# A fused attention and two-MLP kernel: centred tiles turned by VectorE through DRAM, the second MLP ordered behind the next block's first, and bulk transfers issued from GpSimd's queue

## The chip, the cores and the metric

The kernel runs on one NeuronCore of a Trainium2 chip. The metric is the device time of one execution in microseconds (us), lower is better. Matrix products run on TensorE (PE in the profile, its weight loads PEld), elementwise work on VectorE (DVE) and ScalarE (ACT), a little on GpSimd (POOL), and transfers are issued by SyncE (SP). In the kernel before, every transfer is issued by SP.

## The reference

```python
scores = (1 / S) * z @ z.T                     # per batch, B = 2, S = 3136, d_qk = 64
x = u * (relu(scores) ** 2 @ v)                # d_model D = 256
h = relu(x @ w_in)                             # first MLP, d_ff = 1024
c = conv over 3 neighbouring rows of h, one weight per column (conv_w)
x = (h * sigmoid(c)) @ w_out
xn = (x - mean(x)) / sqrt(var(x) + 1e-6) * g_ln    # second MLP
out = x + relu(xn @ w_ch1) @ w_ch2             # 4 * 256 = 1024 wide
```

Inputs and output are float32.

## The kernel before

Every float32 operand is split into a high and a low part (names that end in `h` and `l`), and a product is three matmuls: high by high, high by low, low by high. PE is the engine with the most work.

Attention runs over 14 chunks of 3 or 4 tiles of 128 queries (7 for each batch), and within a chunk over 25 tiles of 128 keys. A score tile `s` is computed by PE, made to `a` by ACT (relu, square), split into `ah` and `al`, and used by six `av` matmuls. Scores are symmetric, so a tile whose mirror image was computed in an earlier chunk is not computed again: `spill` turned it with a DVE transpose into a buffer `bl` and wrote it to a DRAM tensor `turned`, and `land` reads it back in four transfers. Each finished chunk is multiplied by `u` and written to a DRAM tensor `gated` (`x out`).

The MLPs run over 17 blocks of tokens, 15 of 3 x 128 and two of 2 x 128. For each block, `make_x` loads a stretch of `gated` into a tile `x` (`x in`), and ACT and DVE split it into `xh` and `xl`, of which there is one buffer each. `mlps` then issues, for eight slices of d_ff, the `up` matmuls into `hps`, the convolution and the gate on ACT and DVE, and the `down` matmuls into the PSUM tile `y`. The result is copied to `ysb`; the mean and variance come from bn_stats, each row tile is centred into `xn` (`center`), PE turns the six 128 x 128 pieces of `xn` into the PSUM tile `tps` by matmuls with the identity (`turn`, 6 instructions), and ACT and DVE scale them into `xth` and `xtl`. The second MLP is again eight slices of `up` (into `h2ps`) and `down` (into `y`), and the rows are written out. The reciprocal root is applied after the second MLP and runs on POOL (`pow`).

The order of the instructions on each engine is not the order of the code. `Program` records every operation with its engines, a price and a due time, plays them through with those prices, picks the most urgent one that is ready and has room in its buffers, and issues the result. The order is then fixed: every engine, and every queue of transfers, runs its list from the front, and an instruction that has to wait holds up what stands behind it. `when` gives the due times of a block, `LAG0` and `LAG1` how far it lies behind its attention. Where the plan has a gap on PE of over 0.1 us, `fill` puts matmuls on zeros (`warm_ps<-zero`, or `y<-zero` and `av<-zero` where they add zero to a sum), one for each 0.125 us.

Of the kernel before, what the change touches and what calls it, by code (L numbers as in the profile page):

```python
# [8 lines left out]
F32 = mybir.dt.float32  # L9
# [20 lines left out]
LAG0 = 120.0  # L30
LAG1 = 6.0
# [12 lines left out]
REST = 0.9  # L44
FLOAT = ("ACT", "POOL")
# [48 lines left out]
class Program:  # L94
# [62 lines left out]
    def order(self):  # L157
# [17 lines left out]
        done, now, port, owner, moved_at = [], 0.0, 0.0, None, 0.0  # L175
        busy = dict.fromkeys(ENGINES, 0.0)
        while len(done) < len(self.ops):
# [32 lines left out]
            for e in ENGINES:  # L210
# [4 lines left out]
                for o in open_[e]:  # L215
# [3 lines left out]
                    if (e == "POOL" or e == "DVE" and o.port) and port > now + 1e-9 and owner != e:  # L219
                        later(port)  # L220
                        continue
# [22 lines left out]
                if o.kb is not None:  # L244
                    moved_at = max(moved_at, now + us) + o.kb / RATE
                    o.end = moved_at + LANDS + LATE.get(o.name, 0.0)
                if e == "POOL" or e == "DVE" and o.port:
                    port, owner = now + us + 0.06, e
# [49 lines left out]
def attn_moe_kernel(ctx: ExitStack, tc: tile.TileContext, zt, ut, v, w_in, conv_w, w_out, g_ln, w1, w2, out):  # L298
# [28 lines left out]
    def maker(tag, places, where, shape, dtype):  # L327
# [7 lines left out]
        for tag, places, where, shape, dtype in (  # L335
            ("zst", 1, pool, [P, 512], F32),
            ("st", 2, pool, [P, 1024], F32),
            ("bl", 4, pool, [P, CW], F32),
# [10 lines left out]
            ("x", 1, pool, [P, 2 * XW], F32),  # L349
# [6 lines left out]
            ("ysb", 1, pool, [P, NTT * D], F32),  # L356
            ("xn", 3, pool, [P, D], F32),
# [49 lines left out]
    def dma(fn, kb, **kw):  # L407
        return op([("SP", 0.45)], lambda e: fn(), late=LANDS + kb / RATE, kb=kb, **kw)
# [14 lines left out]
    def load_z(b, i, with_lh=None):  # L423
# [3 lines left out]
        dma(lambda: nc.sync.dma_start(out=at(st, "zst")[:, :n], in_=zt[b, :, c0:c1]), n / 2, reads=held(b), writes=[(st, 0)], name="z1" if b else "z")  # L427
# [25 lines left out]
    def load_v(b, j0, j1):  # L453
        st = buf("st")
# [6 lines left out]
        if full > j0:  # L461
            dma(
                lambda: nc.sync.dma_start(
# [3 lines left out]
                128 * (full - j0), reads=held(b), writes=[(st, 0)], name="v1" if b else "v",  # L467
            )
            keys.append((st, 0))
        if j1 == NJ:  # L470
            for o in (0, 64):
                dma(
                    lambda o=o: nc.sync.dma_start(out=tile_()[o : o + 64, full - j0, :], in_=v[b, full * P : S, :]),
                    64, writes=[(st, 1 + o)], name="v",
# [67 lines left out]
    def load_w(nm, i):  # L542
        st = buf("st")
# [5 lines left out]
        def start():  # L549
            if nm in ("wi", "w1"):  # L550
                k, o = divmod(i * 512, DFF)
                nc.sync.dma_start(out=words(), in_=wsrc[nm][:, k, o : o + 512, :])
            else:
                nc.sync.dma_start(
# [10 lines left out]
    def load_cw():  # L565
# [3 lines left out]
            lambda: nc.sync.dma_start(out=at(st), in_=conv_w.bitcast(U32).rearrange("p (n two) -> p n two", two=2)),  # L569
# [10 lines left out]
    def swap_lh(c):  # L580
# [5 lines left out]
        dma(lambda: nc.sync.dma_start(out=f(at(b, "lh")[:64, :n]), in_=f(hl[64:, q0:q1])), 96, reads=keys, writes=[(b, 0)], name="lh")  # L586
# [650 lines left out]
```

## Time and profile before

| | |
|---|---|
| median of 3 runs | 1100.31 us (1099.48 to 1100.45) |
| the profiled execution | 1099.48 us; its span, first to last instruction, 1097.7 us |
| PE busy | 1086.1 us, 99% of the span |
| DVE / ACT / POOL busy | 78% / 66% / 3% of the span |
| granted TensorE clock | full throughout (2.4 GHz) |
| moved by DMA | 115.43 MB, mean 105 GB/s |

Busy time on PE is time in which a matmul is in flight; successive matmuls overlap, so the time that one costs is the distance from its start to the next one's, which is shorter than its duration. A wait is put down to the instruction whose end came last before the waiting one began.

### The profile page before, as it was taken

How to read it: one execution, taken by the hardware profiler on the slowest of the kernel's cores; microseconds unless marked ns; L12 is line 12 of the kernel's file. 1: busy time of each engine (PE TensorE's matmuls, PEld its weight loads, DVE VectorE, ACT ScalarE, POOL GpSimd, SP SyncE). 2: the span in 40 equal slices, each digit the busy share in tenths (PEclk: the TensorE clock that was granted, in tenths of full speed). 3: DMA queues.
4: the chain of work that ended last, by engine and by line, in shares of the span. 5: the costliest groups of instructions: out<-in, count | busy, mean ns of one | idle time of the engine just before them, and what ended most of it. 6: DMA issues, size and time to landing. Idle time of an engine off the chain costs nothing.

```text
span 1097.7 us, 19194 instructions
## 1 busy us (share of the span) xinstructions
PE 1086.1 (99%) x6641; PEld 1023.4 (93%) x6641; DVE 858.9 (78%) x1820; ACT 723.7 (66%) x1506; POOL 32.2 (3%) x48
## 2 busy tenths in 40 slices
PE   8999999999999999999999999999999999999998
PEld 7888988989999989899989999999899999999998
DVE  7999999988778696869694959595849668487973
ACT  7778887865657595858584857484747557355752
POOL 2000000000000000000000000000000000000000
PEclk9999999999999999999999999999999999999999
DMA  6775888776557431213142413340534545450000
GB/s 202 227 197 148 200 184 179 162 161 135 98 134 151 139 88 44 82 44 103 35 106 69 116 37 87 79 91 26 112 87 96 130 84 94 109 83 27 25 15 20
DMA packets 373793, 115.43 MB, mean 105 GB/s; under 512 B 277312, under 2 KB 365376, under 8 KB 373696
## 3 DMA queue, kind: packets, MB, share of 16 engines
q1 hardware_dynamic: 373696, 114.21, 44.2%
q8 instruction: 52, 0.85, 0.3%
q14 instruction: 45, 0.37, 0.1%
HBM read 64.74 MB, written 46.47 MB: 101 GB/s over the span
## 4 chain that ended last, share of the span: by engine, by line
PE 91%; ACT 3%; DVE 2%; DMA 1%; issue 1%; SPq 1%; DVEq 0%; ACTq 0%
PE av L755 12%; PE av L758 12%; PE av L757 11%; PE y L856 8%; PE y L858 8%; PE y L857 8%; PE hps L840 4%; PE h2ps L840 4%; PE hps L841 4%; PE h2ps L842 4%; PE h2ps L841 4%; PE hps L842 4%; PE s L714 3%; PE s L713 3%; PE tps L1014 1%
## 5 line engine op out<-in xcount | busy, mean ns | idle before, releaser
L755 PE MATMUL av<-ah,vh 128*128 128x512 f32 (+2 forms) x700 | 257.8, 368 | 2.9 <-ACT ah L397 1.1
L758 PE MATMUL av<-ah,vl 128*128 128x512 f32 (+2 forms) x700 | 256.0, 366 | 0.0
L757 PE MATMUL av<-al,vh 128*128 128x384 f32 (+2 forms) x672 | 246.7, 367 | 2.2 <-DVE al L692 2.1
L1047 DVE SCALAR_TENSOR_TENSOR g2l<-h2ps,g2h 128x384 fp32r<-128x384 f32 (+1 forms) x136 | 73.3, 539 | 101.2 <-ACT g2h L1042 100.7
L1042 ACT ACTIVATE g2h<-h2ps 128x384 fp32r<-128x384 f32 (+1 forms) x136 | 65.3, 481 | 130.0 <-PE h2ps L842 128.4
L755 PEld LDWEIGHTS av<-ah,vh 128*128 128x128 f32 x700 | 131.6, 188 | 15.1 <-ACT ah L397 1.8
L758 PEld LDWEIGHTS av<-ah,vl 128*128 128x128 f32 x700 | 131.5, 188 | 14.6
L757 PEld LDWEIGHTS av<-al,vh 128*128 128x128 f32 x672 | 126.4, 188 | 14.0 <-DVE al L692 3.9
L722 ACT ACTIVATE a<-s 128x512 f32<-128x512 f32 (+2 forms) x196 | 106.0, 560 | 38.6 <-PE s L714 37.9
L692 DVE TENSOR_TENSOR al<-a,ah 128x512 fp32r<-128x512 f32 (+2 forms) x182 | 114.8, 639 | 9.4 <-ACT ah L397 8.8
L856 PE MATMUL y<-w2h,g2h 128*128 128x256 f32 x392 | 110.0, 281 | 0.6 <-DVE ysb L1057 0.6
L856 PE MATMUL y<-woh,gh 128*128 128x256 f32 x392 | 109.8, 280 | 0.2 <-ACT ysb L948 0.2
L858 PE MATMUL y<-w2h,g2l 128*128 128x256 f32 x392 | 109.7, 280 | 0.0
L858 PE MATMUL y<-woh,gl 128*128 128x256 f32 x392 | 109.7, 280 | 0.0
L857 PE MATMUL y<-w2l,g2h 128*128 128x256 f32 x392 | 109.7, 280 | 0.0
L857 PE MATMUL y<-wol,gh 128*128 128x256 f32 x392 | 109.6, 280 | 0.0
L692 DVE TENSOR_TENSOR al<-land,ah 128x384 fp32r<-128x384 f32 (+2 forms) x154 | 92.3, 600 | 21.7 <-ACT ah L397 16.2
L731 ACT ACTIVATE a<-a 128x512 f32<-128x512 f32 (+2 forms) x183 | 105.8, 594 | 1.4
L397 ACT CAST ah<-a 128x512 fp32r<-128x512 f32 (+2 forms) x181 | 104.2, 587 | 3.3 <-PE av L758 2.2
L635 DVE STREAM_TRANSPOSE bl<-a 128x512 f32<-128x512 f32 (+1 forms) x146 | 94.8, 658 | 11.3 <-ACT a L731 11.0
L906 ACT ACTIVATE t<-t 128x384 f32<-128x384 f32 (+1 forms) x136 | 69.1, 512 | 39.9 <-DVE t L899 39.6
L876 ACT ACTIVATE h<-hps 128x386 f32<-128x386 f32 (+1 forms) x136 | 64.7, 482 | 44.3 <-PE hps L842 43.7
(122 smaller groups left out, 2471.4 us busy)
## 6 DMA issues: line engine op xcount, KB each, us to landing
turned<-bl SPq DMA_DIRECT2D x90, 256.0 KB, 2.5
land<-turned SPq DMA_DIRECT2D x328, 48.0 KB, 2.4
land<-turned SPq DMA_DIRECT2D x168, 56.0 KB, 2.4
turned<-bl SPq DMA_DIRECT2D x44, 192.0 KB, 2.4
land<-turned SPq DMA_DIRECT2D x120, 64.0 KB, 2.5
out_dram<-ysb SPq DMA_DIRECT2D x15, 384.0 KB, 2.7
vst<-in_v_dram SPq DMA_DIRECT2D x11, 512.0 KB, 4.4
x<-gated SPq DMA_DIRECT2D x14, 386.0 KB, 4.0
```

Source lines behind the costliest of these rows:

```text
L397: nc.scalar.copy(dst, src)
L635: [("DVE", price("dve_turn", w))], lambda e: nc.vector.transpose(at(b, "bl")[:, :w], at(ab)[:, :w]),
L692: lambda e: nc.vector.tensor_tensor(at(al, "al")[:, :n], a(), f(at(ah)[:, :n]), ALU.subtract),
L722: [("ACT", price("act_ps", n))], lambda e: nc.scalar.activation(a(), at(ps)[:, :n], AF.Relu),
L731: op([("ACT", price("act", n))], lambda e: nc.scalar.activation(a(), a(), AF.Square), writes=[(ab, 0)], name="square")
L755: nc.tensor.matmul(p, vhj, at(ah)[:, :n], start=first(b, d), stop=False, **kw)
L757: nc.tensor.matmul(p, vhj, at(al)[:, :n], start=False, stop=False, **kw)
L758: nc.tensor.matmul(p, vlj, at(ah)[:, :n], start=False, stop=False, **kw)
L840: nc.tensor.matmul(p, a, h_, start=d == 0, stop=False)
L856: nc.tensor.matmul(p, a, wh, start=first(acc, (i0 + i) // 2), stop=False, **kw)
L857: nc.tensor.matmul(p, a, wl, start=False, stop=False, **kw)
L858: nc.tensor.matmul(p, b, wh, start=False, stop=k == NF - 1, **kw)
```

## The change

Four things change together.

1. For the first 14 blocks (`far`) the centred tile `xn` is no longer turned by PE. DVE turns its 32 x 32 squares (one STREAM_TRANSPOSE of 128 x 768 into `tn`), a transfer from POOL's queue writes `tn` to a DRAM tensor `centred`, and four transfers from SP read it back with the squares in their place, into the buffer of `xtl`. ACT and DVE then make `xth` and `xtl` from SBUF instead of PSUM. The columns lie in another order for that, so the `up` matmuls of these blocks read their moving operand in runs of 32 elements (`woven`). The last three blocks keep PE's transposes.
2. `mlps` is a generator that stops before the second MLP. The loop runs the first part of a block and then the rest of the block before it, and the due times of the second MLP are those of the next block's first, less 0.1 of its length.
3. `dma` takes a flag `bulk`: transfers of `z` and `v` of the second batch, of `u` (but the first), of the weights and small tables, `x out`, `x in` and the output (but those of the last blocks), and `xn out` are issued by POOL on its own queue. `spill`, `land`, `lh` and the first batch's loads stay on SP.
4. The tile `x` is gone: `x in` lands in the one buffer of `xl`, which DVE then overwrites with the low part. So the load for a block starts when the block before has made its last read of `xl`. `bl` goes from 4 buffers to 3, `ysb` from 1 to 2, `xn` from 3 of 128 x 256 to 2 of 128 x 768. LAG0 goes from 120 to 130, LAG1 from 6 to 8, and the staging tiles `st` are handed out in the order of the code.

```diff
-LAG0 = 120.0
-LAG1 = 6.0
+LAG0 = 130.0
+LAG1 = 8.0
+BACK = 0.1
...
-            ("bl", 4, pool, [P, CW], F32),
+            ("bl", 3, pool, [P, CW], F32),
...
-            ("x", 1, pool, [P, 2 * XW], F32),
...
-            ("ysb", 1, pool, [P, NTT * D], F32),
-            ("xn", 3, pool, [P, D], F32),
+            ("ysb", 2, pool, [P, NTT * D], F32),
+            ("xn", 2, pool, [P, NTT * D], F32),
...
-    def dma(fn, kb, **kw):
-        return op([("SP", 0.45)], lambda e: fn(), late=LANDS + kb / RATE, kb=kb, **kw)
+    QUEUE = {"SP": nc.sync, "POOL": nc.gpsimd}
+
+    def dma(fn, kb, bulk=True, **kw):
+        return op([("POOL", 0.75) if bulk else ("SP", 0.45)], lambda e: fn(QUEUE[e]), late=LANDS + kb / RATE, kb=kb, **kw)
...
-        x = buf("x", True)
         xh, xl = x_b[i] = buf("xh", True), buf("xl", True)
+
+        def x(a=0, b=w):
+            return f(at(xl, "xl"))[:, : 2 * w].rearrange("p (k t) -> p k t", k=2)[:, :, a:b]
+
         dma(
-            lambda: nc.sync.dma_start(out=half(x, w, a - s, b - s, "x"), in_=gated[:, :, a:b]),
+            lambda q: q.dma_start(out=x(a - s, b - s), in_=gated[:, :, a:b]),
...
         def when2(x):
-            return when(x) + DEFER[c - NK] if beside else when(x)
+            return when(x) + DEFER[c - NK] if beside else whens[c + 1](x - BACK)
...
+                    if woven:
+                        p = p.rearrange("p (i b k) -> p i b k", b=4, k=SQ)
+                        h_ = h_.rearrange("p (b i k) -> p i b k", b=4, k=SQ)
+                        l_ = at(tl)[:, : 2 * w].rearrange("p (b two i k) -> p two i b k", b=4, two=2, k=SQ)[:, d]
...
+        far = c < NK - 3
+        xn, tn = buf("xn"), buf("xn") if far else None
...
+        if far:
+            xt = tl
+            place = centred[c % 2]
+            op(
+                [("DVE", price("dve_turn", ntt * D))],
+                lambda e: nc.vector.transpose(
+                    at(tn, "tn")[:, : ntt * D].rearrange("p (g j k) -> p j g k", g=4, k=SQ),
+                    at(xn)[:, : NTT * D].rearrange("p (j g k) -> p j g k", g=4, k=SQ),
+                ),
+                reads=[(xn, i) for i in range(ntt)], writes=[(tn, 0)], name="turn", port=True,
+            )
+            dma(
+                lambda q: q.dma_start(out=place.rearrange("b q x -> (b q) x"), in_=at(tn)[:, : ntt * D]),
+                n, reads=[(tn, 0)], writes=[("centred", c % 2)], name="xn out",
+            )
+
+            def fetch(e):
+                for g in range(P // SQ):
+                    nc.sync.dma_start(
+                        out=f(at(xt, "xtl"))[g * SQ : (g + 1) * SQ, : ntt * D].rearrange("p (b x) -> p b x", b=4),
+                        in_=place.rearrange("b q (g x) -> g q b x", g=4)[g],
+                    )
...
+    left = None
+    for i in range(NK):
         make_x(i)
-        mlps(i, when[i])
+        run = mlps(i)
+        next(run)
+        for x in (left,) if i < NK - 3 else (left, run):
+            for _ in x or ():
+                pass
+        left = run if i < NK - 3 else None
```

The order of the instructions shows the change at three places. On PE, in the middle of the run, a block before had its six transposes a few matmuls ahead of its second MLP (`hps` is the first MLP's `up`, `h2ps` the second's, `s` and `av` attention):

```order
2489 L713 MATMUL s<-hl 128x512
2490 L714 MATMUL s<-lh,hl 128x512
2491 L1014 MATMUL tps<-ident,xn 128x128 x6
2492 L755 MATMUL av<-ah,vh 128x512
2493 L757 MATMUL av<-al,vh 128x512
2494 L758 MATMUL av<-ah,vl 128x512
2495 L840 MATMUL hps<-xh,wih 128x386
...
2500 L840 MATMUL h2ps<-xth,w1h 128x384
```

In the changed kernel a second MLP begins with no transposes, and the next block's `down` matmuls of the first MLP (`y<-woh`) stand beside it:

```order
2357 L765 MATMUL av<-ah,vl 128x512
2358 L857 MATMUL h2ps<-xth,w1h 128x384
2359 L858 MATMUL h2ps<-xtl,w1h 128x384
2360 L859 MATMUL h2ps<-xth,w1l 128x384
...
2364 L873 MATMUL y<-woh,gh 128x256
2365 L874 MATMUL y<-wol,gh 128x256
2366 L875 MATMUL y<-woh,gl 128x256
```

The 84 `tps` rows of the first 14 blocks are gone from the list, and the second MLP has moved behind a whole first MLP.

On the queues, SP's list before held the loads of `x` and the output between the spills (`turned<-bl`):

```order
149 L790 DMA x<-gated 128x2x386
150 L643 DMA turned<-bl 128x4x128 x6
151 L1064 DMA out_dram<-ysb 128x3x256
152 L643 DMA turned<-bl 128x4x128 x4
153 L790 DMA x<-gated 128x2x386
154 L643 DMA turned<-bl 128x4x128 x6
155 L1064 DMA out_dram<-ysb 128x3x256
```

Now they stand on POOL, in one list with the `pow` of each block (`rs<-ve,mhalf`) and the writes of the turned tiles:

```order
92 L800 DMA xl<-gated 128x2x386
93 L1004 TENSOR_TENSOR rs<-ve,mhalf 128x3
94 L1038 DMA centred<-tn 128x768
95 L1133 DMA out_dram<-ysb 128x3x256
96 L800 DMA xl<-gated 128x2x386
97 L1004 TENSOR_TENSOR rs<-ve,mhalf 128x3
98 L1038 DMA centred<-tn 128x768
99 L1133 DMA out_dram<-ysb 128x3x256
```

What moved: a load of `x` no longer waits behind spills, but it waits behind POOL's other rows and behind PE's last read of `xl`.

At the start of the run, PE's list before held two fill matmuls (`warm_ps<-zero`) between the score tiles that follow the first long run of `av` matmuls:

```order
40 L713 MATMUL s<-hl 128x512
41 L714 MATMUL s<-lh,hl 128x512
42 L1163 MATMUL warm_ps<-zero 128x256 x2
43 L713 MATMUL s<-hl 128x512
```

The list of the changed kernel holds 8 at the same place, and 8 more six `av` matmuls later:

```order
42 L720 MATMUL s<-hl 128x512
43 L721 MATMUL s<-lh,hl 128x512
44 L1235 MATMUL warm_ps<-zero 128x256 x8
45 L762 MATMUL av<-ah,vh 128x512
...
50 L765 MATMUL av<-ah,vl 128x512
51 L1235 MATMUL warm_ps<-zero 128x256 x8
```

Over the whole list the fill matmuls go from 95 to 112: in the first tenth from 64 to 92, in the middle from 12 to 1, at the end 19 in both.

## Rows read from the trace of the kernel before

**Rows 1.** The page: span, PE's busy time, the chain that ended last by engine.

```profile
span 1097.7 us, 19194 instructions
...
PE 91%; ACT 3%; DVE 2%; DMA 1%; issue 1%; SPq 1%; DVEq 0%; ACTq 0%
```

**Rows 2.** Busy us by stretch: length, PE, PEld, DVE, ACT, POOL, clock, DMA share, GB/s.

```profile
0.00:25.00 25.00, 22.08 (x104) 18.42 (x105) 18.60 (x34) 18.36 (x35) 6.98 (x15) 1.00 0.73 222
...
225.00:250.00 25.00, 22.42 (x134) 20.97 (x134) 22.26 (x48) 16.39 (x35) 0.00 (x0) 1.00 0.77 166
...
1000.00:1098.00 98.00, 92.95 (x729) 91.87 (x728) 66.04 (x176) 50.10 (x125) 2.52 (x4) 1.00 0.07 21
```

**Rows 3.** The same view for one stretch.

```profile
25.00:225.00 200.00, 199.45 (x1010) 175.84 (x1009) 189.40 (x369) 162.81 (x332) 7.68 (x12) 1.00 0.74 180
```

**Rows 4.** PE's waits, first and last of seven: total us, times, longest.

```profile
PE av L757 <- DVE al L692: 2.1, 4, 1.6
...
PE y L856 <- ACT ysb L948: 0.2, 1, 0.2
```

**Rows 5.** The chain that ended last, in order of time: start us, us, what.

```profile
227.22 3.48 DMA land<-turned
...
288.50 0.66 PE tps L1014 x6
...
1065.92 2.04 PE y L1163 x17
```

**Rows 6.** PE in order of time, 284 to 289 us: start us, us, what.

```profile
284.30 0.34 PE L755 MATMUL av<-ah,vh 128*128 128x384 f32 x1
284.48 0.34 PE L757 MATMUL av<-al,vh 128*128 128x384 f32 x1
...
288.34 0.82 PE L1014 MATMUL tps<-ident,xn 128*128 128x128 f32 x6
```

**Rows 7.** PE in order of time, 7 to 12 us.

```profile
7.67 1.60 PE L1163 MATMUL warm_ps<-zero 128*128 128x256 f32 x12
9.11 0.39 PE L755 MATMUL av<-ah,vh 128*128 128x512 f32 x1
```

**Rows 8.** Groups by line and shape: count, busy us, mean ns, idle before.

```profile
L840 PE MATMUL hps<-xh,wih 128*128 128x386 f32 x240 | 82.1, 342 | 0.0
...
L840 PE MATMUL h2ps<-xth,w1h 128*128 128x384 f32 x240 | 81.0, 338 | 0.0
...
L882 ACT ACTIVATE t<-h,cw 128x384 f32<-128x384 f32 x120 | 74.4, 620 | 5.6 <-DVE gl L922 4.3
...
L635 DVE STREAM_TRANSPOSE bl<-a 128x512 f32<-128x512 f32 x96 | 66.5, 702 | 9.8 <-ACT a L731 9.7
...
L635 DVE STREAM_TRANSPOSE bl<-a 128x384 f32<-128x384 f32 x50 | 28.3, 571 | 1.5 <-ACT a L731 1.2
...
L806 DVE TENSOR_TENSOR xl<-x,xh 128x386 fp32r<-128x386 f32 x30 | 16.5, 556 | 0.8 <-ACT xh L397 0.7
...
L1022 ACT ACTIVATE xth<-tps,gt 128x384 fp32r<-128x384 f32 x30 | 16.3, 583 | 1.4 <-PE tps L1014 1.4
...
L397 ACT CAST xh<-x 128x386 fp32r<-128x386 f32 x30 | 14.9, 510 | 0.5 <-DMA x<-gated 0.5
```

**Rows 9.** The tile x: its issue on SP (ns min/median/max), its landing.

```profile
L790 SPq DMA_DIRECT2D x<-gated x17: 542/566/1547, 66.3 to 1022.4; - x17
...
DMA to landing us min/median/max: 3.1/3.8/6.3
```

**Rows 10.** Issues of transfers: count, KB each, median us to landing.

```profile
out_dram<-ysb SPq DMA_DIRECT2D x15, 384.0 KB, 2.7
...
lh<-hl SPq DMA_DIRECT2D x12, 96.0 KB, 2.5
```

**Rows 11.** Waits of ACT for transfers, the two longest in total.

```profile
ACT ah L397 <- DMA land<-turned: 12.1, 12, 2.6
...
ACT hl L397 <- DMA zst<-in_zt_dram: 5.9, 3, 3.0
```

More of the change, by code (lines that the diff above doesn't have):

```diff
@@ L174, in order @@
                 enter(o)
-        done, now, port, owner, moved_at = [], 0.0, 0.0, None, 0.0
+        done, now, port, owner, moved_at = [], 0.0, 0.0, None, {"SP": 0.0, "POOL": 0.0}
         busy = dict.fromkeys(ENGINES, 0.0)
@@ L218, in order @@
                         continue
-                    if (e == "POOL" or e == "DVE" and o.port) and port > now + 1e-9 and owner != e:
+                    if (e == "POOL" and o.kb is None or e == "DVE" and o.port) and port > now + 1e-9 and owner != e:
                         later(port)
@@ L244, in order @@
                 if o.kb is not None:
-                    moved_at = max(moved_at, now + us) + o.kb / RATE
-                    o.end = moved_at + LANDS + LATE.get(o.name, 0.0)
-                if e == "POOL" or e == "DVE" and o.port:
+                    x = "POOL" if e == "SP" else "SP"
+                    t = max(moved_at[e], now + us)
+                    took = o.kb / RATE
+                    took += min(took, max(0.0, moved_at[x] - t))
+                    moved_at[e] = t + took
+                    o.end = t + took + LANDS + LATE.get(o.name, 0.0)
+                if e == "POOL" and o.kb is None or e == "DVE" and o.port:
                     port, owner = now + us + 0.06, e
@@ L952, in mlps @@
             )
-        xns = []
         for i in range(ntt):
@@ L1008, in mlps, with source, target @@
         over = [("hl", i, x) for i in range(2) for x in "hl"] if c == NK - 2 else []
[L1009 to L1019 removed]
+        if far:
[19 more added lines that the diff above has]
+                    )
+            op(
+                [("SP", 2.05)], fetch, late=LANDS + n / RATE, kb=n, reads=[("centred", c % 2)], writes=[(xt, "in")],
+                name="xn in",
+            )
+            def source(d):
+                return f(at(xt))[:, : ntt * D].rearrange("p (b two x) -> p two b x", b=4, two=2)[:, d]
+            def target(t, d):
+                if t is th:
+                    return half(t, n, name="xth")[:, d, :].rearrange("p (b x) -> p b x", b=4)
+                return at(t)[:, : ntt * D].rearrange("p (b two x) -> p two b x", b=4, two=2)[:, d]
@@ new lines, in mlps, with turn, source, target @@
+        for d in range(2):
+            if far:
+                got = (xt, "in")
+            else:
+                ps = buf("w", kind="m")
+                got = (ps, 0)
+                def turn(e, d=d, ps=ps):
+                    for i in range(ntt):
+                        nc.tensor.transpose(
+                            at(ps, "tps")[:, i * P : (i + 1) * P], at(xn)[:, (d * NTT + i) * P : (d * NTT + i + 1) * P], ident
+                        )
+                op(
+                    [("PE", ntt * 0.109)], turn, reads=[(xn, i) for i in range(ntt)] + [("ident",)], writes=[got],
+                    due=when(TURN), name="turn",
+                )
+                def source(d, ps=ps):
+                    return at(ps)[:, :n]
+                def target(t, d):
+                    return half(t, n)[:, d, :]
@@ L1067, in mlps @@
                 ),
-                128 * (b - a), reads=[(y, i0 + i) for i in range(a, b)], due=when2(1.1), name="out",
+                128 * (b - a), bulk=c < NK - 2, reads=[(y, i0 + i) for i in range(a, b)], due=when2(1.1), name="out",
             )
```

103 lines of the change are left out of this document (48 added, 55 removed).

## The prediction

> **What bounds the kernel now.** I read the page first. The span is 1097.7 us and PE makes 91% of the chain that ended last [rows 1]; the profiled execution took 1099.48 us, so 1.8 us lie around the span, and it stands 0.83 us under the median of 1100.31. Busy time alone proves little, since matmuls overlap, so I went on to PE's waits: seven kinds, 6.9 us in all, the largest 2.1 us and the smallest 0.2 [rows 4]. Then the stretches: PE is idle for 2.9 us of the first 25 us, 2.6 us of 225 to 250 and 5.0 us of the last 98, the 4 us after its last matmul among them [rows 2]; in the 200 us between the first two it is idle for 0.55 us, although DVE is busy for 189.40 of them [rows 3]. So PE's list of matmuls is the time. A matmul taken out of it is worth its distance to the next start, and nothing that ACT, DVE or a queue saves is worth anything while PE's operands come in time. What can go wrong is that they stop doing so.
>
> **The transposes (removed).** The chain has a block's six transposes as one piece of 0.66 us [rows 5]. PE in order of time agrees: they begin at 288.34, and 0.82 us is the piece with the last one's tail, which the next matmul overlaps, as an `av` matmul of 0.34 us is followed after 0.18 [rows 6]. Fourteen blocks lose them: 14 x 0.66 = **-9.2 us**. Nothing else on PE is removed.
>
> **The fills (moved).** The order of the changed kernel has 112 matmuls on zeros instead of 95. Twelve of them took from 7.67 to the next start at 9.11, 0.12 us each [rows 7], and 17 took 2.04 us at the end [rows 5]. They stand where the plan sees PE waiting, and PE runs them whether it would wait or not: 17 x 0.12 = **+2.0 us**. It is 28 more at the start, which is the price of a start in which more has to arrive, and 11 fewer later.
>
> **The moving operand in runs of 32 (changed).** The 672 `h2ps` matmuls of these blocks (14 x 8 x 6) now read it in twelve runs instead of one. No row has such a read. From below: 0, since columns and output are the same. From above, by the nearest row, a length that is no multiple of 32: 386 columns last 342 ns where 384 last 338 [rows 8], 4 ns, 672 x 0.004 = 2.7 us. I take **0**, because the run is still 32 elements long, and keep 2.7 us for the range.
>
> **The turn by DVE and DRAM (added).** A transpose of 384 elements takes 571 ns and of 512 takes 702 [rows 8], 1.02 ns an element, so about 0.96 us for 768 and 13.5 us for 14. The trip is then the write (2.7 us by a write of the same 384 KB), four reads (2.5 us by transfers of 96 KB [rows 10]), and `xth` from SBUF, where the nearest ACT row with a scale is 620 against 583 ns from PSUM [rows 8]. That is under 10 us with the issues. What hides it is the new order: a second MLP starts a whole first MLP later. Between the last `y<-woh` of a block and its first `h2ps` the changed list holds at least 33 us of matmuls at the distances above. DVE's 13.5 us fall where it has room, except in 25 to 225 us (95% busy [rows 3]), and there only the first block or two are turned while block 0's second MLP moves out. **0**. Without that cover the trip would cost PE some 10 us a block.
>
> **The load of x without a buffer of its own.** This is where cover is thin. Before, `x` was fetched while `xl` was still in use. Now the load starts after PE's last read of `xl`, and PE's next block waits for issue 0.57, landing 3.8 [rows 9], `xh` 0.51 and `xl` 0.56 us [rows 8], 5.4 us in all. In the changed list the matmuls between the last `hps` of a block and the first of the next give PE 7.2 us of other work at the tightest of the thirteen places with a load by POOL, then 8.9, and 12 or more at the eleven others (the tightest of the last blocks' loads, which SP issues, has 5.9). So with SP's numbers it is hidden, by 1.8 us at POOL's tightest place.
>
> **The queue.** No row has a transfer issued by POOL. From below: SP's numbers, and then nothing is lost. From above: the longest landing of `x`, 6.3 against 3.8 us [rows 9], 2.5 us late on each of 14 loads. ACT runs its list from the front, so a late `x` also holds up the score work behind it. How much of an ACT wait reaches PE: ACT waited 12.1 us for `land` and 5.9 for `z` [rows 11], and PE waited 6.9 us for everything [rows 4], so at most 0.38 us per us, and 14 x 2.5 x 0.38 = 13 us at the worst. I take 0.3 us late, by SP's end, which is **+1.5 us**. The Trainium skill, in "DMA: Bandwidth & Descriptors", section "Latency and other measured facts", puts the first byte at about 1 us on GpSimd's path and 0.6 on SyncE's; no run here shows it yet, and by its 0.4 us the term would be 2.1.
>
> **What SP gains.** The stall at 225 to 250 us hangs on a `land` of 3.48 us [rows 5] that was issued among weight loads. With these on another queue and the second MLP's start moved out of the stretch, part of its 2.6 us should go; between 0 and 2.6 I take **-1 us**. The same page, section "Issuing engines are not separate DMA queues", says that the transfers share the same 16 engines and only issue time is saved; by that this term would be 0. Three `bl` buffers instead of four are costed at nothing: a spill occupies one for a transpose of 0.6 us [rows 8], an issue of about 0.6 [rows 9] and a landing of about 2.5 [rows 10], 3.7 us or 1.2 for each of three, and key tiles with a score are at least 1.4 us apart on PE, eight matmuls of 0.18 [rows 6]; if a landing takes 2 us longer, that cover is gone and DVE waits for a buffer.
>
> **Sum.** 1099.5 - 9.2 + 2.0 + 0 + 0 + 1.5 - 1.0 = 1092.8 us for an execution like the profiled one; I forecast **1093 us**.
>
> **The rivals.**
> *More is regained.* The idle of the start (2.9 us) and of 225 to 250 (2.6) goes too and POOL costs nothing: 1099.5 - 9.2 + 2.0 - 5.5 = 1087. Against it: the 28 extra fills say that the start gets harder.
> *Thin cover.* `x` arrives 1 to 1.5 us later than the order allows, 14 x 0.38 = 5.3 us per us of lateness, or the runs of 32 cost their 2.7 us and `x` is half as late: 1092.8 - 1.5 + 5.3 to 8 = 1097 to 1099.5. For it speaks the 1.8 us of room; against it, that eleven of the thirteen places have at least 7 us more than the chain needs.
> *VectorE holds up POOL's transfers.* If POOL can't make a transfer while DVE runs certain instructions, every load of `x` waits for a gap in DVE's work, which is 95% busy early on and 78% over the run. Five DVE instructions of 0.55 us in a row are 2.75 us on 14 loads: 14 x 2.75 x 0.38 = 14.6, and 1092.8 - 1.5 + 14.6 = 1106, slower than before. It decides from 1.6 us of lateness per load (8.2 us eaten), and gives slower than 1102.5 from 2.1 us. Against it: the large cover at most places, so that 0.38 is a ceiling. The skill's "SBUF — State Buffer", section "SBUF: two separate sides", has this as a trap: while DVE runs a two-port mode, GpSimd can't write the descriptors of its transfers. No row of before can show it.
> *The change doesn't do what it says.* Excluded: the order shows no transposes in the 14 blocks and the second MLPs behind the next first ones.
>
> **How the numbers follow.** Forecast 0.60 (1088.5 to 1097), more regained 0.09, thin cover 0.18 (half of it under 1098), VectorE or another cause that makes POOL's transfers very late 0.13. The range is 1087 to 1102, from the best case to where the slow rival begins. About 0.2%, 2.2 us, is what a measurement of this kernel can tell from no change; faster is below 1098.1 us: 0.60 + 0.09 + 0.08 = 0.77; within 0.2%: 0.11; slower: 0.12.
>
> **What would show it.** Right: 14 `tps` rows left, the `h2ps` matmuls still at 338 ns, PE's waits together under 10 us, ACT's `xh` hardly waiting for the load, and POOL's landings of `x` near 4 us. Wrong: PE waiting in front of `hps` for `xh` or `xl` at many blocks, landings of 7 us or more, `land` late on SP because it stands behind a read of `centred` that waits for POOL's write, or `h2ps` matmuls 10 ns further apart, 672 x 0.0108 = 7.2 us being enough to eat the gain.

## The result, and the profile after

The changed kernel takes **1108.59 us** (median of 4 runs, 1107.37 to 1109.86), the kernel before 1099.89 (4 runs): ratio **1.0091 (1.0076 to 1.0105)**, slower. The forecast was 1093 us. The profiled execution took 1107.87 us with a span of 1106.1, 8.4 more than before. First the page's span and the chain that ended last, by engine; they answer to [rows 1]:

```profile
span 1106.1 us, 19378 instructions
PE 87%; DMA 4%; DVE 4%; SPq 2%; ACT 1%; issue 1%; DVEq 0%; POOL 0%; ACTq 0%; POOLq 0%
```

PE still ends the run, but its share of the chain fell from 91 to 87%, and DMA's rose from 1 to 4%. The waits of PE (total us, times, longest), which answer to [rows 4], name two places:

```profile
PE av L762 <- ACT ah L401: 5.9, 3, 3.7
PE s L720 <- DVE hl L441: 3.9, 3, 3.2
...
PE av L762 <- DVE u L780: 1.0, 2, 0.7
```

And the stretches, with the columns of [rows 2]:

```profile
0.00:25.00 25.00, 20.56 (x91) 17.82 (x92) 14.84 (x33) 13.72 (x26) 5.54 (x15) 1.00 0.59 179
...
225.00:250.00 25.00, 24.37 (x147) 23.80 (x146) 22.59 (x49) 18.54 (x43) 3.48 (x4) 1.00 0.69 139
250.00:275.00 25.00, 23.14 (x131) 22.43 (x130) 20.02 (x50) 15.81 (x36) 3.70 (x5) 0.93 0.74 153
275.00:300.00 25.00, 21.94 (x127) 20.09 (x125) 18.39 (x39) 11.90 (x26) 3.59 (x6) 1.00 0.81 168
300.00:325.00 25.00, 23.47 (x128) 22.27 (x129) 16.25 (x30) 13.17 (x26) 4.10 (x6) 0.86 0.86 195
```

PE is idle for 4.4 us of the first 25 (2.9 before), and from 250 to 325 for 6.5 us, where the kernel before had it busy throughout. The granted clock is 0.86 to 0.93 in two of these stretches, so part of the matmuls there ran at the lower level. What the removal was to bring did come: 14 `tps` rows are left of 98, and the turn on DVE takes 970 ns, as worked out (0.96). The groups by line and shape, which answer to [rows 8]:

```profile
L1071 PE MATMUL tps<-ident,xn 128*128 128x128 f32 x14 | 2.2, 272 | 0.0
...
L1031 DVE STREAM_TRANSPOSE tn<-xn 128x768 f32<-128x768 f32 x14 | 13.6, 970 | 1.9 <-ACT xn L987 1.7
```

To see all that PE loses, I took from the trace the distance from each matmul's start to the next one's, as the prediction prices them, and called what lies above the usual distance of its shape a stall:

| | before | after | us |
|---|---|---|---|
| 98, now 14 transposes | 9.0 us | 1.2 us | -7.8 |
| 95, now 112 fills | 11.4 us | 13.4 us | +2.0 |
| stalls, first 25 us | 4.3 us | 8.0 us | +3.7 |
| stalls, 225 to 325 us | 3.9 us | 14.2 us | +10.3 |
| stalls elsewhere | 7.4 us | 4.5 us | -2.9 |
| 2352 `y` matmuls, mean distance | 116.7 ns | 117.9 ns | +2.7 |
| 720 `h2ps` of 384 columns | 174.9 ns | 176.8 ns | +1.4 |
| 720 `hps` of 386 columns | 177.1 ns | 176.4 ns | -0.5 |

The sum is +8.9 for a span that grew by 8.4. A stall in this sense is waiting and slow matmuls together: of the 14.2 us from 225 to 325, somewhat over 4 are matmuls at the lower clock behind the two longest waits, and of the 3.7 that the start loses, about 2.5 are matmuls with longer distances. So four things had to be explained: the start, the stretch at 225 to 325 us, the fills, and two distances.

**The start.** The trace in order of time, start and duration, with what ended the engine's idle time:

```profile
1.55 0.74 POOL L575 DMA_DIRECT2D cst<-in_conv_w_dram  x1 [0.15 <-issue]
...
6.72 0.22 ACT L519 ACTIVATE wc<-cst 128x24 f32<-128x24 f32 x1 [4.71 <-DMA cst<-in_conv_w_dram]
...
6.86 0.60 ACT L401 CAST hl<-zst 128x512 fp32r<-128x512 f32 x1
...
9.07 0.80 PE L720 MATMUL s<-hl 128*128 128x512 f32 x1 [3.25 <-DVE hl L441]
```

The table of the convolution, 24 KB, stands at the head of the lists of ACT and DVE, ahead of the first piece of `z`. POOL issued it at 1.55 us and ACT had it at 6.72; the cast of `z`, whose load SP issued first of all, stands behind it. PE's first score matmul starts at 9.07 us, after an idle time of 3.25, and the ones after it take 0.63 us, where the same matmuls take 0.39 to 0.40 in e1 below. In the kernel before, the first one started earlier:

```profile
5.47 0.50 PE L713 MATMUL s<-hl 128*128 128x512 f32 x1
```

**225 to 325 us.** The chain of that stretch, in order of time:

```profile
251.60 6.17 DMA land<-turned
...
265.83 4.00 DMA land<-turned
...
281.55 3.85 DMA turned<-bl
...
293.75 7.06 DMA land<-turned
300.91 0.58 ACT ah L401
301.53 0.74 PE av L762
```

PE waits for `ah`, and `ah` for the reads of mirrored tiles. SP did little but issue them, back to back:

```profile
233.95 21.57 SPq L667 DMA_DIRECT2D land<-turned  x36
255.62 1.45 SPq L592 DMA_DIRECT2D lh<-hl  x1
257.17 23.19 SPq L667 DMA_DIRECT2D land<-turned  x40
```

But late issue is not all of it here. The two longest waits, which end at 258.56 and 301.53 us, stand on reads that landed after 6.17 and 7.06 us, where 2.4 to 2.7 is usual, and at both places POOL had loads and a write in flight. Around the second one:

```profile
292.44 0.70 POOL L786 DMA_DIRECT2D gated<-u  x1 [10.92 <-DVE u L780]
...
293.88 0.79 POOL L469 DMA_DIRECT2D vst<-in_v_dram  x1
...
296.66 0.72 POOL L606 DMA_DIRECT2D u<-in_ut_dram  x1 [1.98 <-DMA gated<-u]
```

### The profile page after: what moved, and what is told of

It reads as the page before. It is cut to its first block, busy times and chain, and to the rows that moved or that the text cites. A ratio compares the mean times of both kernels' runs of the same rounds, so it can differ in the third digit from the quotient of the medians.

```text
span 1106.1 us, 19378 instructions
## 1 busy us (share of the span) xinstructions
PE 1089.1 (98%) x6574; PEld 1025.9 (93%) x6574; DVE 870.8 (79%) x1830; ACT 731.3 (66%) x1514; POOL 99.9 (9%) x146
## 4 chain that ended last, share of the span: by engine, by line
PE 87%; DMA 4%; DVE 4%; SPq 2%; ACT 1%; issue 1%; DVEq 0%; POOL 0%; ACTq 0%; POOLq 0%
PE av L762 11%; PE av L765 11%; PE av L764 11%; PE y L873 8%; PE y L874 8%; PE y L875 8%; PE h2ps L857 4%; PE h2ps L858 4%; PE hps L859 4%; PE h2ps L859 4%; PE hps L857 4%; PE hps L858 4%; PE s L720 3%; PE s L721 3%; DMA land<-turned 3%; SPq L667 2%
## 5 line engine op out<-in xcount | busy, mean ns | idle before, releaser
L699 DVE TENSOR_TENSOR al<-a,ah 128x512 fp32r<-128x512 f32 (+2 forms) x182 | 114.4, 635 | 11.4 <-ACT ah L401 10.1
L401 ACT CAST ah<-land 128x384 fp32r<-128x384 f32 (+2 forms) x139 | 75.9, 547 | 33.0 <-DMA land<-turned 25.8
```

The costliest lines, as they stand in the source:

```text
L401: nc.scalar.copy(dst, src)
L699: lambda e: nc.vector.tensor_tensor(at(al, "al")[:, :n], a(), f(at(ah)[:, :n]), ALU.subtract),
```

## The experiments

The theory after the first four runs, **C**: with the second MLP moved out, PE has less other work at 200 to 300 us, runs through the mirrored key tiles of the attention faster than SP can issue four reads for each, and waits. The rivals: **A**, two queues that share the transfers make the reads late; **H**, the transfers themselves are slow; **D**, the new order is what hides the trip through DRAM, so that undoing it costs more; **D'**, the transfers of the turned `xn` (`centred`) on SP's queue are what stalls. The expectations of e1 to e4 were written before C and speak of A and a theory B, in their own words.

**e1: the same order, all transfers on SP.**

```diff
-    QUEUE = {"SP": nc.sync, "POOL": nc.gpsimd}
+    QUEUE = {"SP": nc.sync, "POOL": nc.sync}
```

> The changed kernel with the same planned order of every engine, but POOL's transfers are issued by SP, at their places in the planned order. Theory A (bulk transfers on a queue of their own share the DMA engines with the small reads of land, which then take up to 8.3 us): PE's stall between 225 and 325 us falls from about 13 us of lost time to under 6, landings of land stay under 6.5 us, 1100 to 1104 us. Rival B (the lands are issued too late by the order itself, whatever queue carries the bulk): the stall stays or grows, because SP now also waits for what the bulk transfers wait for, 1108 us or more.

1102.96 us, ratio 1.0046 (1.0031 to 1.0061), 5.6 less than the changed kernel. The stall of the first 25 us falls from 8.0 to 3.6: SP issues `cst` at 1.20 us and ACT has it at 3.81. From 225 to 325 it stays at 13.9, so A falls as the cause of the sum, although the time is one that A had forecast. The waits are of another kind, though: ACT's longest for `land` is 3.5 us instead of 5.7. With one queue, then, the stretch loses as much, in more and shorter waits.

**e2: the table's work on ACT and DVE put behind the first score tiles.**

```diff
+    order = (
+        [o for o in order if o.start < AFTER_US and o not in early]
+        + early
+        + [o for o in order if o.start >= AFTER_US]
+    )
```

> The changed kernel with the first few instructions that decode the conv weights moved behind the first score tiles in the lists of ACT, DVE and POOL; the transfers are as they were. Theory S (at the start ACT and DVE stand at the head of their lists before a small table that lands 5.2 us after POOL issued it, while the first z tile is there at 3.6 us): the first score matmul starts at 5.5 to 6 us instead of 9.1, TensorE's clock does not fall at 9 us, and the time falls by 3 to 5 us, to 1104 to 1105.5. Rival (the first z tile itself lands late beside POOL's transfers): the first score stays after 8 us and the time moves by less than 1.5 us.

1106.28 us, 1.0072 (1.0055 to 1.0089): 2.3 us come back, where 3 to 5 were expected; the start's stall goes from 8.0 to 5.9. The first score matmul starts at 5.47 us, as in the kernel before, but PE then waits 1.25 us in front of `av` at 11 us, and from 25 to 225 us its stall grows from 2.5 to 4.7. The table is about half of the start's loss. The rest I didn't separate.

**e3: the moving operand in one run again.**

```diff
-            ... in up(ps, "w1", k, th, tl, n, when2(TURN + 0.02 + UP2 * k / NF), far):
+            ... in up(ps, "w1", k, th, tl, n, when2(TURN + 0.02 + UP2 * k / NF), False):
```

> The changed kernel with the moving operand of the second MLP's up matmuls read in one run of 384 instead of runs of 32; the columns then belong to other tokens, so the second MLP's values are left wrong, and nothing else changes. Theory W (the short runs set the starts of these 672 matmuls 2 to 3 ns further apart): the mean distance goes from 176.9 back to about 174 ns and the time falls by 1.5 to 2 us, to about 1106.8. Rival (the wider distances come with the new order or with POOL's activity, since the y matmuls have them too): the distance stays at 176.5 or more and the time within 0.8 us of 1108.6.

1106.76 us, 1.0078 (1.0059 to 1.0098). The edit leaves the columns with the wrong tokens. The distance of `h2ps` goes from 176.8 to 175.3 ns, and 672 x 1.5 ns = 1.0 us is what the runs of 32 cost. `y` stays at 117.9, so its distance has another cause.

**e4: everything on SP, and planned so.**

```diff
-        return op([("POOL", 0.75) if bulk else ("SP", 0.45)], lambda e: fn(QUEUE[e]), ...)
+        return op([("SP", 0.45)], lambda e: fn(QUEUE[e]), ...)
```

> The changed kernel planned anew with every transfer on SP: the turn through DRAM, the order of the MLPs, the buffers and the lags stay. If the queue is what costs (A and S together): 1092 to 1098 us, faster than before, with the gain of the 84 transposes showing. If the cost lies in the trip through DRAM, in the load of x without its own buffer or in the new order of the MLPs: 1104 us or more, with PE waiting for xh, xl or xth.

1096.84 us (10 runs), 0.9986 (0.9976 to 0.9995). The queue, then, costs 11.7 us inside the change (11.5 by the ratios): 5.6 by its issuing (the changed kernel against e1) and 6.1 by the order that is planned for it (e1 against e4: 16 fewer fills, 2 us, and 4.7 us less stall). ACT still waits for `land` from 200 to 350 us, and PE stalls 7.4 us from 225 to 350: about 4 up to 325, as in the kernel before, and the rest behind it.

**e5 to e7: one part alone.** e5 and e7 give the second MLP its old place:

```diff
-            return when(x) + DEFER[c - NK] if beside else whens[c + 1](x - BACK)
+            return when(x) + DEFER[c - NK] if beside else when(x)
...
-        for x in (left,) if i < NK - 3 else (left, run):
+        for x in (run,):
```

e5 does it with everything on SP, e7 with the two queues. e6 keeps the new order, with everything on SP, and sets `far = False`. All three keep the lags, the buffers and the load into `xl` of the changed kernel, so what those cost is inside their times and was not separated.

> One part of the change alone: the centred tiles of 14 blocks are turned by DVE and DRAM, but a block's second MLP stays right behind its first, with the first's due times, and SP issues everything. Theory C (with the second MLP moved behind the next first one, PE has no second MLP to do from 200 to 300 us, runs through the attention faster than SP can issue the four reads of each key tile, and waits for them): without the new order the stretch 225 to 350 us stalls no more than in the kernel before (about 4 us), the 84 transposes save 8 to 9 us, and if the trip through DRAM is still covered the time is 1090 to 1094. Rival D (the new order is what hides the trip): PE waits for xth in front of h2ps, up to 10 us at each of 14 blocks, and the time is 1100 or more, up to 1200. On the distance between starts of y matmuls, 116.7 ns before and 117.9 after: if the new order causes it, 116.7 here; if the layout of the turned tiles does, 117.9.

> The other part alone: the second MLP stays behind the next block's first, PE does the transposes of all blocks (98 rows of tps again), SP issues everything. Theory C: the stall from 225 to 350 us stays (6 us or more, as in the run with everything on SP), nothing is saved on the transposes, so about 1096.8 + 8.5 = 1105, 1102 to 1108. Rival D': the order itself costs nothing and e4's stall comes from the writes and reads of the turned tiles on SP's queue: no stall above 4 us from 225 to 350 and a time within 0.2% of before, 1097 to 1101.

> The changed kernel with its two queues, but with a block's second MLP right behind its first. Theory C: the start still loses 3 to 4 us against before (the table of the convolution at the head of ACT's and DVE's lists, and the first loads on POOL's queue), but 225 to 325 us does not stall beyond 5 us; 1094 to 1098 us. Rival A (sharing of the transfers by two queues makes the reads of the mirrored tiles late whatever the order): the stretch 225 to 325 still loses 10 us or more, 1103 or later.

e5: 1134.51 us, 1.0322 (1.0307 to 1.0338). e6: 1113.87, 1.0136 (1.0120 to 1.0153). e7: 1127.27, 1.0254 (1.0239 to 1.0270). The times that I expected of e5 and e7 from theory C are far off: without the new order the trip through DRAM isn't covered. The plan sees PE waiting and fills, 291 fills in e5 and 211 in e7 against 96 in e4, and some waits remain, as the largest of e5:

```profile
PE h2ps L857 <- ACT xth L1088: 4.1, 1, 4.1
```

e6, with 150 fills, lies above its 1102 to 1108 too. D holds: the turn needs the order, and the order without the turn loses 15 us; only together (e4) do they gain. What C says of the reads is half borne out: ACT's waits for them fall when the order is undone (8.4 us in e7, 13.8 in e5, against 20.6 after and 24.4 in e4), though PE is slower there for other reasons too. They stay at 21.8 in e6, which has no transfers of `centred` at all and still stalls 8.5 us from 225 to 325. D' falls by that.

**e8, e9: the queue alone.** The kernel before with `bulk` transfers on POOL and the planner's model of two queues; e9 also hands out the staging tiles in the order of the code.

> The kernel before with one part of the change: the bulk transfers on POOL's queue, planned with that queue; transposes by PE, old order, the tile x in its own buffer. It is the price of the queue by itself. The prediction's term was +1.5 - 1 = +0.5 us: 1099 to 1101. By the accounts of the runs so far it is the start's: stall of the first 25 us 8 instead of 4.3 us and a dozen more fills, so +4 to +6: 1103 to 1105, with no more stall than before from 225 to 325 us.

> The price of POOL's queue by itself, once more: the kernel before with its bulk transfers on POOL's queue, and with the staging tiles st handed out in the order of the code as in the changed kernel (without that the weights took them ahead of v, which e8 shows). Old order, transposes by PE, x in its own buffer. Its list holds 125 fill matmuls where the kernel before has 95: 30 x 0.12 = 3.6 us. Theory F (the queue costs about 6 us by fills, by the late tables of the start, and by POOL's transfers being later): 1103 to 1108 with 7 to 9 us of stall in the first 25 us and no worse stall than before at 225 to 350 us. The prediction's term: 1099 to 1101.

e8: 1184.97 us, 1.0783 (1.0767 to 1.0799). Without an order for `st`, POOL loads weights into the staging tiles ahead of `v`, and PE fills for 75 us:

```profile
26.39 74.80 PE L1169 MATMUL warm_ps<-zero 128*128 128x256 f32 x622
```

With it (e9) 1104.70 us, 1.0054 (1.0041 to 1.0068): the queue costs 5.9 us in the old order. It is 30 fills (3.6 us), 3.0 us more stall in the first 25 and 1.7 more from 25 to 225, less the stall at 225 to 250, which is gone:

```profile
225.00:250.00 25.00, 25.00 (x161) 25.00 (x160) 22.84 (x50) 16.93 (x37) 2.32 (x4) 1.00 0.74 153
```

**e11: inputs on SP, x and the outputs on POOL.** `bulk=False` for `z`, `v`, `u`, the weights and the tables.

> The changed kernel with all loads of inputs (z, v, u, weights, tables) back on SP and planned so; POOL keeps x out, x in, the writes of the turned tiles and the output. Fills in the list: 97 (112 in the changed kernel). Theory F (of the queue's 11.7 us, the larger part is the start and the plan that goes with input loads on POOL, not POOL's transfers of x): first 25 us stall 4 to 5 us as before, time 1096 to 1099. Rival G (POOL's late transfers of x and of the turned tiles hold up the blocks): start as before but 1101 to 1106, with waits of ACT for xl in at many blocks. In either case ACT still waits over 15 us for land between 200 and 350 us, because the order is kept.

1099.67 us, 1.0002 (0.9992 to 1.0012). The start is as before (3.7 us of stall) and 97 fills are left. So of the queue's 11.7 us about 9 are the input loads, and POOL's loads of `x`, writes and outputs cost 2.8 (1.8 by the ratios).

**e13, e15: what makes the reads late.** e13 lets POOL issue the four reads of every second mirrored tile. e15 keeps e4's order and fetches a tile by one read:

```diff
-            for o in range(P // SQ):
-                nc.sync.dma_start(
-                    out=at(b, "land")[o * SQ : (o + 1) * SQ, :n].rearrange("p (g k) -> p g k", k=SQ),
-                    in_=blocks_[o, :, g0 : g0 + n // SQ, :],
-                )
+            nc.sync.dma_start(
+                out=at(b, "land")[:, :n].rearrange("p (g k) -> p g k", k=SQ),
+                in_=rows.rearrange("(g q) (b k) -> (q b) g k", q=SQ, k=SQ),
+            )
```

> As e4, but the four reads of every second mirrored key tile are issued by POOL instead of SP, and planned so (103 fills in the list, 96 in e4, which is 0.8 us more). From 200 to 350 us ACT waits 24 us for land in e4 and SP is busy issuing 22 of every 25 us. Theory C (SP's issue of four reads per key tile is what the new order runs into): ACT's waits for land fall below 12 us, PE's stalls from 225 to 350 us from 8.3 to under 5 us, time 1093 to 1096. Rival H (the reads are late because of the transfers themselves, or POOL's pow and slower issue hold its reads up): the waits stay at 20 us or more and the time is 1097 or more.

> The order of e4 to the instruction, but a mirrored key tile is fetched by one read of the same bytes in the same pieces instead of four; its rows come out in another order across the partitions, so the values of attention are wrong. It takes away three quarters of what SP has to issue, and leaves the transfers. Theory C (SP's issue of the reads is what the new order runs into from 200 to 350 us): ACT's waits for land there fall from 24 to under 8 us, PE's stalls from 225 to 375 us from 8.3 to under 4 us, time 1090 to 1094. Rival H (the transfers themselves are late): waits of 18 us or more, and 1096 or more. e13 spoke for C by a dose upward: POOL's reads started 1.75 us apart instead of 0.52 and landed in the same 2.4 to 2.6 us, and the run took 1152 us.

e13: 1152.10 us, 1.0477 (1.0453 to 1.0501). POOL's list ran far slower than its price: the median distance between starts of its reads is 1.75 us (0.52 on SP), though one lasts 632 ns. The issues, with KB each and median us to landing:

```profile
land<-turned SPq DMA_DIRECT2D x168, 48.0 KB, 2.5
land<-turned POOLq DMA_DIRECT2D x160, 48.0 KB, 2.4
```

They land as fast as SP's. As a relief for SP this didn't work: ACT waits 47.1 us for `land` from 200 to 350 us, which is what H said of POOL's slower issue. What it does show is how much hangs on the rate of issue. e15, which leaves the rows of a tile in another order across the partitions: **1088.84 us**, 0.9910 (0.9897 to 0.9924), 8.0 less than e4. ACT has no wait for `land` left from 200 to 375 us, though a read now lands in 3.4 to 4.1 us instead of 2.3 to 2.6, and PE's stalls from 225 to 375 us go from 8.9 to 2.0 us. In the windows of e15 PE is as good as never idle where the changed kernel loses most:

```profile
250.00:275.00 25.00, 25.00 (x156) 25.00 (x156) 23.64 (x56) 18.64 (x42) 1.74 (x2) 1.00 0.98 224
275.00:300.00 25.00, 24.74 (x144) 23.75 (x143) 18.09 (x39) 12.95 (x27) 0.00 (x0) 1.00 0.67 123
300.00:325.00 25.00, 25.00 (x159) 24.14 (x158) 23.63 (x49) 18.65 (x39) 0.00 (x0) 1.00 0.84 181
```

C holds for e4's stall and H falls there: it is the number of reads that SP must issue. The changed kernel itself was not run with one read, so for its long landings H is not excluded. What C missed is that giving the order up costs more.

**e10, e12, e14: the same order at other addresses.** All have e4's order to the instruction; only buffers are a little longer, so that the tiles behind them move (the addresses are those of the compiled program).

```diff
-            ("xh", 1, pool, [P, 2 * XW], F32R),
+            ("xh", 1, pool, [P, 2 * XW + 8], F32R),
...
-            ("bst", 2, pool, [P, NTT, 6], F32),
+            ("bst", 2, pool, [P, NTT + 2, 6], F32),
```

This is e14's edit; e10 gives each buffer of `h` 14 columns more, and e12 also gives 8 to `t` and 12 to `bst`.

> The order of e4 (everything on SP) to the instruction, with one tile size changed: each of the three buffers of h is padded from 386 to 400 columns, so that gh, gl and the tiles behind them lie 96 bytes further. In the kernel before gh began at 32 bytes past a multiple of 64, in the changed kernel and in e4 at a multiple of 64, now at 32 again. Theory E (the distance between starts of y matmuls, 116.7 ns before and 117.9 in every run that has the changed tiles, comes from where the weights that PE loads lie): 116.7 here, 2350 x 1.2 ns = 2.8 us less than e4, 1093 to 1094.5. Rival: the distance has another cause, it stays at 117.9 and the time at 1096.8.

> Again the order of e4 to the instruction, with other tile sizes: each buffer of h, t and bst is 32 bytes longer, so that gh and gl begin 64 bytes (modulo 128) from wo, as in the kernel before, and xth and xtl 64 bytes from w1. So far the distance between starts of the y matmuls was 116.7 ns where gh - wo is 64 modulo 128 (the kernel before, e8, e9), 117.9 where it is 32 (the changed kernel, e4), 119.1 where it is 0 (e10); and the h2ps matmuls in runs of 32 had 176.7 where xth - w1 is 32 or 96 and 175.7 where it is 64 (e10). Theory E2 (the place of the two operands relative to each other in 128 bytes sets the distance): y 116.7, h2ps 175.7, so 2350 x 1.2 + 670 x 1.0 = 3.5 us less than e4: 1093 to 1094. Rival: it was chance or another tile; y stays at 117.9 or more and the time at 1096 or more.

> e12 gave y 117.4 and 117.5 ns and h2ps 176.8: the addresses matter (117.9, 119.1 and 117.5 with one and the same order), but the rule of 128 bytes was wrong. Now xh is 32 bytes longer and bst 64, so that gh, gl, g2h and g2l begin at 352 modulo 512 exactly as in the kernel before, and xth at 352 modulo 512 as in e10, where h2ps was at 175.7. The order is e4's to the instruction. If only the place modulo 512 of the loaded weights matters: y 116.7, h2ps 175.7, 2350 x 1.2 + 670 x 1.0 = 3.5 us less than e4, 1093 to 1094. If it hangs on more than that, y is anywhere from 116.7 to 119 and the time moves by 2.35 us for each ns of it.

| | `gh` modulo 512 | `y`, mean distance | `h2ps` | time | ratio |
|---|---|---|---|---|---|
| before | 352 | 116.7 ns | 174.9 ns (not in runs of 32) | | 1 |
| e4 | 320 | 117.9 | 176.7 | 1096.84 us | 0.9986 (0.9976 to 0.9995) |
| e10 | 416 | 119.2 | 175.7 | 1099.19 | 1.0005 (0.9996 to 1.0014) |
| e12 | 480 | 117.5 | 176.8 | 1096.72 | 0.9981 (0.9972 to 0.9990) |
| e14 | 352 | 116.2 | 175.8 | **1093.43** | **0.9951 (0.9938 to 0.9965)** |

The rows of one group show it too, in the changed kernel, e10 and e14:

```profile
L875 PE MATMUL y<-woh,gl 128*128 128x256 f32 x392 | 110.4, 282 | 0.0
```

```profile
L875 PE MATMUL y<-woh,gl 128*128 128x256 f32 x392 | 110.8, 283 | 0.3 <-DVE gl L939 0.3
```

```profile
L875 PE MATMUL y<-woh,gl 128*128 128x256 f32 x392 | 109.6, 280 | 0.5 <-DVE gl L939 0.5
```

My first guess (modulo 64) was wrong in e10, the second (relative place modulo 128) in e12. With `gh` where it lay before modulo 512, the distance is back. It is one run, and other tiles moved with `gh`, so the rule behind it isn't shown. e14 leaves nothing out and is faster than both kernels.

## Why the prediction was wrong

**The step that failed is "What SP gains".** It took the stall at 225 to 250 us to shrink by 1 us, because weight loads leave SP's queue and the second MLP's start moves out of the stretch. The first half is right, and worth more than I took: in the old order the queue alone removes that stall (e9). The second half has the wrong sign. The second MLP was what PE did while SP issued reads. From 200 to 250 us the next block's first MLP takes its place (`hps`), but from 250 to 300 both are short. `h2ps` matmuls by stretch and then `hps`, before (columns as in [rows 2], PE's first):

```profile
200.00:250.00 50.00, 8.67 (x42) 7.33 (x42) 3.56 (x7) 3.46 (x7) 1.00 0.76 160
250.00:300.00 50.00, 5.72 (x30) 5.22 (x30) 3.09 (x6) 2.47 (x5) 1.00 0.62 123
```

```profile
200.00:250.00 50.00, 2.70 (x12) 2.04 (x12) 1.00 (x2) 1.00 0.76 160
250.00:300.00 50.00, 6.55 (x30) 5.15 (x30) 2.47 (x5) 1.00 0.62 123
```

and after:

```profile
200.00:250.00 50.00, 0.00 (x0) 0.00 (x0) 0.00 (x0) 0.00 (x0) 1.00 0.76 164
250.00:300.00 50.00, 5.23 (x24) 4.26 (x24) 2.11 (x4) 1.94 (x4) 0.97 0.77 160
```

```profile
200.00:250.00 50.00, 9.94 (x48) 8.26 (x48) 3.96 (x8) 1.00 0.76 164
250.00:300.00 50.00, 1.37 (x6) 1.09 (x6) 0.49 (x1) 0.97 0.77 160
```

The `av` matmuls from 250 to 300 us, which use the mirrored tiles, before and after:

```profile
250.00:300.00 50.00, 26.23 (x134) 22.55 (x132) 0.00 (x0) 1.00 0.62 123
```

```profile
250.00:300.00 50.00, 30.95 (x154) 26.09 (x152) 1.11 (x2) 0.97 0.77 160
```

From 250 to 300 us PE had 30 `up` matmuls of the MLPs (24 and 6) where it had 60, and took 154 instead of 134 `av`. SP issued the 40 reads from 257 us 0.58 us apart, so the four of a tile take it 2.3 us, while the six `av` of the tile take PE 1.2 us at 0.20 each: SP keeps up only while PE has about as much other work. It was no freer in the kernel before:

```profile
269.95 23.70 SPq L660 DMA_DIRECT2D land<-turned  x40
```

ACT's waits for these reads from 200 to 350 us follow the order. Before, after, and with the order but neither turn nor second queue (e6):

```profile
ACT ah L397 <- DMA land<-turned: 5.8, 5, 2.6
```

```profile
ACT ah L401 <- DMA land<-turned: 20.6, 13, 5.7
```

```profile
ACT ah L401 <- DMA land<-turned: 21.8, 21, 3.2
```

Instead of -1 the stretch cost +10.3. From 225 to 375 us PE stalls about 4 us in the kernel before, 1.2 with the queue alone (e9), 8.9 with the order and turn on SP (e4) and 14.2 with all of it. The order, with its lags and buffers, costs about 5, and the queue, which by itself takes the stall away, adds about 5 more to the order. For the first 5, e15 shows that the issue of the reads is the cause. The second 5 stay when SP issues everything in the order planned for two queues (e1, 13.9), so they go with that plan, though by other waits there. How far the long landings beside POOL's transfers and the lower clock behind the waits set them in the changed kernel is not shown.

**The queue, +1.5 us**, failed too, and by the runs it is the larger miss: 5.9 alone and 11.7 in the change, its part in the stretch above among them. It was sized by the loads of `x`, and those behaved: 14 issues of 712 to 756 ns, the prediction's landings "near 4 us":

```profile
xl<-gated POOLq DMA_DIRECT2D x13, 386.0 KB, 4.3
```

ACT's `xh` waited for them 1.0 us in all, and PE never waited in front of `hps`. What was missing from the sum is the input loads at the head of the run (3.7 us of stall, about half of it by the 24 KB table) and what the planner does with POOL's prices. Without the queue and with `gh` where it lay, e14 takes 1093.43 us. That this is the forecast is luck: the stall that the order adds, which the sum didn't have, stands there in place of fills and a queue that it did have.

**Fills, +2.0**: right to the tenth, 112 at 0.12 us. **Transposes, -9.2**: right in kind, 7.8 in size, because the chain's 0.66 us for six is above the mean distance of 0.55. **The turn, 0**: right, and e5, where that cover is gone, took 37.7 us more than e4, 2.7 us a block where the prediction had some 10. **The load of `x`, 0**: right. **Runs of 32, 0**: 1.0 us, inside the bound of 2.7. The `y` matmuls were not in the sum, since nothing in the diff touches them; their tiles moved, +2.7 us. Of the signs of being right, one did not come: PE's waits together are 12.7 us and not under 10.

**The rivals.** 1106 us for "VectorE holds up POOL's transfers" is close to the time, for another reason: the issues and landings of `x` above leave no room for 2.75 us a load. The page "SBUF — State Buffer" of the Trainium skill, section "SBUF: two separate sides", says that POOL can't write descriptors while DVE runs a two-port mode. The changed kernel's 14 issues of `x`, 712 to 756 ns with DVE 79% busy, show no sign of it. e13's reads on POOL do start late, but DVE's TENSOR_TENSOR and SCALAR_TENSOR_TENSOR cover about 60% of the issues' time and of the gaps' alike, so that trace doesn't point at them either; its cause stays open. The Trainium skill's "DMA: Bandwidth & Descriptors", section "Issuing engines are not separate DMA queues", by which only issue time is saved, would have given SP's gain as 0. In this case issue time was worth 8.0 us (e15 against e4), and what a second issuer saved in the old order (e9) was not saved in the new one.

Open: the rest of the start's loss beside the table, what the queue adds to the stall in the new order, what of an address sets the `y` distance, and why POOL's reads start 1.75 us apart.

## What to carry to other kernels

When a block of work is moved away from a stretch, ask what that work was covering there: a queue that was just fast enough beside it can become the bound, so count the issues against the matmuls of that stretch beforehand. A second queue is not free at the head of a run, where one small table at the head of two engines' lists held up the first tiles by 3.6 us (9.07 against 5.47). And a change that resizes buffers moves others: compare the distances of untouched matmuls before a loss is put down to the edit, since here two paddings were worth 3.4 us.

## What the runs showed of the hardware

- The mean distance between `y` matmuls was 116.2 to 119.2 ns with one and the same order, by the place of the tiles in SBUF alone (e4, e10, e12, e14).
- POOL issued a load of 386 KB in 734 ns, and it landed in 4.3 us; SP took 566 and 3.8 in the kernel before [rows 9]. POOL's reads of 48 KB in rows of 32 elements started 1.75 us apart in the median, against 0.52 on SP (e13).
- A moving operand in twelve runs of 32 elements cost 1.5 ns on a matmul of 384 columns (e3).
- After 3.68 us without a matmul, PE's `av` matmuls of 448 columns started 0.37 us apart and lasted 0.57 to beyond 306 us, where those ahead of the gap started 0.20 us apart; the granted clock of 300 to 325 us is 0.86, so the lower level (1.2 of 2.4 GHz) was granted there for a time:

```profile
301.53 0.74 PE L762 MATMUL av<-ah,vh 128*128 128x448 f32 x1 [3.68 <-ACT ah L401]
...
303.10 0.57 PE L762 MATMUL av<-ah,vh 128*128 128x448 f32 x1
303.48 0.57 PE L764 MATMUL av<-al,vh 128*128 128x448 f32 x1
```
